# Computing qkv with the seven-product scheme of the first feed-forward matrix, and passing it to attention through DRAM

## The chip, the cores and the metric

The kernel runs on one core of a Trainium2 chip. A core has a matrix engine (PE), two engines for elementwise work (VectorE, in the profile DVE, and ScalarE, ACT), a general one (GpSimd, POOL), and a queue engine (SyncE, SP) that here does nothing but issue DMAs. The time is device microseconds of one execution, and a kernel's time is the median of its runs. Of the kernel before, three runs took 1124.48, 1124.85 and 1126.0 us.

## The reference

One transformer block over 2048 tokens of width 576, attention and feed-forward in parallel:

```
xn  = layernorm(x)
qkv = xn @ wqkv                      # 576 x 1728: q, k, v of 32 heads of 18
    # token s attends to s, s-2, ..., s-14 (8 keys, dilation 2)
    # logits * 18**-0.5, keys before token 0 masked, softmax
out = x + attention(q, k, v) @ wo + relu(xn @ w1) @ w2     # w1: 576 x 4608
```

All is float32 and is computed as such: every operand of a matrix product is split into a high and a low part (fp32r), and a product is three matmuls, high by high, low by high, high by low.

## The kernel before, in words

**Tiles.** The dilation is 2, so even and odd tokens never meet in attention. The kernel takes them as two phases of 1024 tokens; a phase is 8 tiles of 128 tokens, and a half is 4 tiles, 512 tokens. The width 576 is four blocks of 128 rows and a rest of 64.

**Feed-forward.** The 4608 hidden units are 36 tiles of 128, taken as 18 pairs. A pair and a half of the tokens is a product of a 2x2 block matrix by a 2x2 block matrix (tokens in two groups of 256 columns, hidden units in two tiles), and is done with seven block products (P1 to P7 in `pstep`) rather than eight. The weights stand still in PE and the tokens move, 256 columns in a matmul; 50 matmuls make one pair for one half. The seven slots of weights, sums and differences of the blocks, come from `set_make`: it loads a pair from a packed copy in DRAM (`w1c`), and VectorE and ScalarE form the differences in `ts` and the split parts in one of two buffers `wset`. The results are relu-ed and split by ScalarE (`hhi`) and VectorE (`hlo`), and multiplied by w2 in what is called an o-step here (`o_step`, six matmuls of 256 and 320 columns), which adds into the residual in `po`. The first pair's products are plain ones of 14 matmuls (`classic`).

**qkv.** The 32 heads are four units of 8 heads, 144 columns of each of q, k and v. In `qkv_tile` the tokens stand still in PE and the weights move: for one tile of 128 tokens and one unit, 14 matmuls of 432 columns give k, v and q with tokens on partitions. ScalarE copies the three out of the bank in three operations, into `kk`, `v` and `qo`. Four units, eight tiles and two phases make 64 such tiles. The tiles of a unit are placed between the products of one pair, at pairs 0, 3, 7, 11 and 1, 4, 8, 12 of the two phases.

**Attention.** VectorE does it, unit by unit: multiply (`pr<-qo,kk`), reduce, softmax, multiply by v, add. `kk` and `v` hold 15 slots of 144 columns on each of 128 partitions: seven slots of keys that come before the phase's tile order, then the eight tiles. Tile i and partition p is token 8p+i of the phase; the seven slots ahead hold the keys of the partition below. They are filled by the halo (`halo`, line 950): a copy within SBUF, of slots 8 to 14 of partitions 0 to 126 into slots 0 to 6 of partitions 1 to 127. It is issued as two DMAs, of 112 and of 15 partitions:

```
HALO = ((0, 112), (112, 127))
            send(lambda z=z, a=a, b=b: nc.sync.dma_start(z[a + 1 : b + 1, 0 : W - 1, :], z[a:b, NI : NI + W - 1, :]), 250, BANK["pm"])
            for z in (k, v) for a, b in HALO
```

**Order.** Every engine runs its instructions in the order written. A planner in the kernel (`Order`) writes it: it keeps a clock per engine from simple costs, puts an operation where its inputs are due, and puts attention's work on VectorE into the room that is left (`later`). `send` issues a DMA on SP's queue; an issue that waits holds every later issue of SP. `keep` puts work on POOL at the moment it is planned; the packed copies of weights are made there, by a one-element copy (`spare<-hhi`) that waits for something recent, and a DMA behind it.

Of the kernel before, what the change touches and what calls it, by code (L numbers as in the profile page):

```python
# [16 lines left out]
P = 128  # L17
# [9 lines left out]
NCL = 1  # L27
QP = ((0, 3, 7, 11), (1, 4, 8, 12))
WOP = ((5, 9, 13, 16), (6, 10, 14, 17))
HALO = ((0, 112), (112, 127))  # L30
# [12 lines left out]
class Op:  # L43


    __slots__ = ("eng", "dur", "fn", "after", "due", "end", "lag", "then")

    def __init__(self, eng, dur, fn, after, due, lag=0.0):
        self.eng, self.dur, self.fn, self.due, self.lag = eng, dur, fn, due, lag
        self.after = [a for a in after if a is not None]  # L50
        self.end = None
        self.then = None


class Order:
# [14 lines left out]
    def ready(self, op):  # L70
        r = 0.0
        for a in op.after:
            if a.end is None:
                return None
            r = max(r, a.end)
        return r

    def give(self, op, start):
        op.fn()
        self.clk[op.eng] = start + op.dur  # L80
        op.end = start + op.dur + TAIL[op.eng] + op.lag
        if op.then:
            op.then.end = self.gp = max(self.gp, op.end) + op.then.dur

# [111 lines left out]
def tile_body(ctx: ExitStack, tc: tile.TileContext, x, wqkv, wo, w1, w2, out):  # L196
# [13 lines left out]

    ctx.enter_context(tc.manual_schedule())
# [6 lines left out]
    hp = pool("hp", 5)  # L218
    whp = pool("whp", 2)
    pad3 = pool("pad3", 1).tile([P, PADS[3]], F32, name="pad3")  # L220
    vp = pool("vp", 2)
    prp = pool("prp", 2)
    lgp = pool("lgp", 1)
    smp = pool("smp", 2)
# [19 lines left out]
    BUF = [keep.tile([P, 2, 2176], F32R, name=f"wset{b}") for b in range(2)]  # L244
# [12 lines left out]
    VLAST = [[], []]  # L257

    def v_turn(last):

        o_.force(VLAST.pop(0))
        VLAST.append(last)

    def v_tile(last=None):
        v_turn([] if last is None else last)
        return vp.tile([P, 2176], F32, name="v")[:, 0 : (W - 1 + NI) * UD].rearrange("p (w c) -> p w c", w=W - 1 + NI)

    def wset(m):
        z = BUF[m % 2][:, :, 0:2048]
        return z.rearrange("p e (s k c) -> p e s k c", s=8, k=2)  # L270

    def wqset(p):
        z = BUF[(p + 1) % 2].rearrange("p e c -> p (e c)")
        return z[:, 0 : 10 * 3 * UD].rearrange("p (e t c) -> p e t c", e=2, t=5)
# [6 lines left out]
    QO, rr, RD = [None, None], [None, None], [None, None]  # L281
# [151 lines left out]
    WQC = [dram.tile([D, 3, UD], F32, name=f"wqc{u}") for u in range(NU)]  # L433
# [37 lines left out]
    TSGOT = {}  # L471

    def set_early(m):

        src = W1C[m % NP][0:256, P : 2 * P].rearrange("(k p) c -> p k c", p=P)
        TSGOT[m] = send(lambda: nc.sync.dma_start(TS[:, 1], src), 128, [*kept["w1", m % NP], *ts_free[0]])

    def set_make(m, fine=False):

        n = m % NP  # L480
        late = 0.0 if fine or m == 2 else 4.0
        aside = 5 if NP - 2 <= m < NP + 3 else 0
        w = wset(m)
        z = f32(w)[:, 1]
        got = {}
        free = slots_free(m % 2, range(8))

        def rest_rows():
            for rows in slice(0, DR), slice(DR, P):
                got[RR] = send(  # L490
                    lambda rows=rows: nc.sync.dma_start(z[rows, RR].rearrange("p k c -> p (k c)"), W1C[n][KT * P : D, :]),
                    64, [*kept["w1", n], *free], late,
                )

        for rows, f, s in ((0, 0, B11), (0, 1, B12), (256, 1, B22), (256, 0, B21)):
            if s == B12 and m in TSGOT:
                got[s] = TSGOT.pop(m)
                rest_rows()
                continue
            ts = s == B12  # L500
            dst = TS[:, 1] if ts else z[:, s]
            src = W1C[n][rows : rows + 256, f * P : (f + 1) * P].rearrange("(k p) c -> p k c", p=P)
            got[s] = send(
                lambda dst=dst, src=src: nc.sync.dma_start(dst, src), 128, [*kept["w1", n], *free, *(ts_free[0] if ts else [])], late
            )
            if s == B12:
                rest_rows()
        ok = {}

        def parts(a, b, step, src, after, slack):  # L510
            v = slice(a, b + 1, step)
            z = hi_lo(w[:, 0, v], w[:, 1, v], src, 256 * (1 + (b - a) // step), after, slack)
            for q in range(a, b + 1, step):
                ok[q] = z

        c1 = dve(lambda: sub(TS[:, 0], TS[:, 1], z[:, B11]), 256, [got[B12], got[B11]], 3 if fine else 5)
        if fine:
            parts(B11, B11, 1, z[:, B11 : B11 + 1], [got[B11], c1], 3.3)
            parts(T1, T1, 1, TS[:, 0:1], [c1], 4)
            parts(RR, RR, 1, z[:, RR : RR + 1], [got[RR]], 4.5)  # L520
        c3 = dve(lambda: sub(TS[:, 1], z[:, B22], TS[:, 1]), 256, [got[B22], c1], 5.1)
        c2 = dve(lambda: sub(TS[:, 2], z[:, B22], TS[:, 0]), 256, [c1, c3], 5.2)
        c4 = dve(lambda: sub(TS[:, 3], z[:, B21], TS[:, 2]), 256, [got[B21], c2], 5.3)
        if fine:
            parts(T2, T2, 1, TS[:, 2:3], [c2], 5.6)
            parts(B21, B21, 1, z[:, B21 : B21 + 1], [got[B21], c4], 6)
            parts(T3, T3, 1, TS[:, 1:2], [c3], 7)
            parts(B22, B22, 1, z[:, B22 : B22 + 1], [got[B22], c2, c3], 8)
            parts(T4, T4, 1, TS[:, 3:4], [c4], 9)
        else:  # L530
            parts(T1, T3, 4, TS[:, 0:2], [c1, c3], 9 + aside)
            parts(T2, T4, 4, TS[:, 2:4], [c2, c4], 10 + aside)
            parts(B11, B21, 2, z[:, B11 : B21 + 1 : 2], [got[B11], got[B21], c1, c4], 11 + aside)
            parts(B22, RR, 2, z[:, B22 : RR + 1 : 2], [got[B22], got[RR], c2, c3], 12 + aside)
        ts_free[0] = [*ok[T1], *ok[T3], *ok[T2], *ok[T4]]
        SETOK[m] = ok
# [4 lines left out]
    def w2_make(m, f):  # L541
        W2[m, f] = w = w2p.tile([P, 2, D], F32R, name="w2t")
        g = send(lambda: nc.sync.dma_start(f32(w[:, 1]), W2C[m % NP][f * P : (f + 1) * P]), 295, kept["w2", m % NP], 4.0)
        W2OK[m, f] = hi_lo(w[:, 0], w[:, 1], f32(w[:, 1]), D, [g], (24 if NP <= m < NP + 3 else 12) + 2 * f)

    WQOK = {}

    def wq_make(p, u, kts, raw=None, hold=None):

        w = wqset(p)  # L550
        b = (p + 1) % 2
        v = wqkv.rearrange("r (s c) -> r s c", s=3)[:, :, u * UD : (u + 1) * UD] if raw is not None else WQC[u]
        for kt in kts:
            z = raw[:, kt] if raw is not None else f32(w)[:, 1, kt]
            after = [] if raw is not None else list(kept["wq", u])
            free = slots_free(b, range(432 * kt // 256, min(7, (432 * kt + 431) // 256) + 1))
            if raw is None:
                after += free
            z3 = z.rearrange("p (s c) -> p s c", s=3)
            if kt < KT:  # L560
                g = [send(lambda: nc.sync.dma_start(z3, v[kt * P : (kt + 1) * P]), 221, after)]
            else:
                g = [send(lambda rows=rows: nc.sync.dma_start(z3[rows], v[KT * P : D]), 110, after)
                     for rows in (slice(0, DR), slice(DR, P))]
            if hold is not None:
                hold.append((kt, w[:, 0, kt], w[:, 1, kt], z, g))
                continue
            WQOK[p, kt] = hi_lo(w[:, 0, kt], w[:, 1, kt], z, 3 * UD, [*g, *free], 5 if p == NP + 1 else 2.5)
# [3 lines left out]
    def wo_make(ph, u):  # L572
        if u < NU:
            WO[ph, u] = w = qop[u % 2].tile([P, 2, D], F32R, name=f"qo{u % 2}")
        else:
            v_turn([])
# [3 lines left out]
        if u < NU:  # L580
            got.append(send(lambda: nc.sync.dma_start(z, WOC[u * UD : u * UD + P, :]), 295, [*kept["wo",], *turned[ph, u], *OFREE[u % 2]], 3.0))
        else:
            for b in (0, DR):
                for v in range(NU):
                    got.append(send(
                        lambda b=b, v=v: nc.sync.dma_start(z[b + 16 * v : b + 16 * v + 16], WOC[v * UD + P : (v + 1) * UD, :]),
                        37, kept["wo",], 3.0,
# [10 lines left out]
    T8 = 8 * 0.1135  # L598

    def h_alloc(key):  # L600
        H[key] = hp.tile([P, TBN], F32R, name="hhi"), hp.tile([P, TBN], F32R, name="hlo")

    def h_parts(key, src, after, slack, alloc=True):

        def high():
            h_alloc(key)
# [7 lines left out]
        a = act(high, TBN, after, slack)  # L614
        b = dve(low, TBN, [a], slack + 0.45)
        HOK[key] = [a, b]
        return [a, b]

    def terms(o, ws, xs, start):
        for j, (wp, xp_) in enumerate(((0, 0), (0, 1), (1, 0))):  # L620
            for k in range(len(ws[0])):
                mm(o, ws[wp][k], xs[xp_][k], start and j == k == 0, False)

    def rest(bank, m, f, xr):
        w = wset(m)
        for e in range(2):
            mm(bank, w[:, e, RR, f], xr, False, e == 1)

    def slot(m, s):
        w = wset(m)  # L630
        return [[w[:, e, s, k] for k in range(2)] for e in range(2)]
# [8 lines left out]
    def classic(g, j, f, name):  # L640
        ph, n, h = G[g]
        m = g // 2
# [5 lines left out]
        def f_():  # L648
            cnt = 0
            for wp, xp_ in ((0, 0), (0, 1), (1, 0)):  # L650
                for hf in range(2):
                    for k in range(2):
                        mm(bank[:, 0:TBN], first[hf][wp][k], a[hf][xp_][k], cnt == 0, False)
# [4 lines left out]
        t = pe(f_, 14 * 0.1135, [*ok[ks[0]], *ok[ks[1]], *ok[RR], *XOK[h, j], *BANK[name]])  # L658
        BANK[name] = h_parts((g, j, f), bank[:, 0:TBN], [t], 0.8)
        SETFREE[m % 2] = {q: t for q in range(8)}  # L660
# [25 lines left out]
    def pstep(g, name):  # L686
        ph, n, h = G[g]
        m = g // 2
        n2, n3 = ("bk2", "bk3") if g % 2 else ("bk3", "bk2")
# [730 lines left out]
```

## Time and profile before

| | |
|---|---|
| runs | 1124.48, 1124.85, 1126.0 us |
| span of the profiled execution, first to last instruction | 1122.7 us |
| instructions | 22406 |
| PE busy | 1116.2 us, 99% |
| VectorE busy | 825.5 us, 74% |
| ScalarE busy | 760.0 us, 68% |
| GpSimd busy | 213.1 us, 19% |
| granted PE clock, mean | 0.999 |
| DMA | 138972 packets, 115.64 MB |

The span is 1.8 to 3.3 us below the three runs; the profiled execution's own time is not listed apart from its span. In rows of groups stand the line of the kernel, the engine, the operation, output<-inputs, the shape and count, then total busy time and mean of one in ns, and the idle time before it with what ended it. Rows of the timeline and of the chain start with a start and a length in us. Most operations are recorded by helpers, so one line number (L304 matmul, L301 VectorE, L298 ScalarE) stands for many places; the tile names tell them apart.

### The profile page before, as it was taken

To read this page: it belongs to the slowest core of one execution; us is meant where nothing else is said; L and a number is where in the kernel's file an instruction comes from. 1 tells how busy PE (TensorE), PEld (TensorE's weight loads), DVE (VectorE), ACT (ScalarE), POOL (GpSimd) and SP (SyncE) were. 2 spreads that over 40 slices of the span, in tenths; PEclk is the share of its full clock that TensorE was granted. 3 is DMA by queue.
4 is the path that set the end of the run, shared out by engine and by line. 5 is a ranking of instruction groups with operands and counts; after the bars stand their busy time and mean duration, and the time that the engine had idled before them with its cause. 6 is when DMAs were issued, how large, how long until landed. Compare 5 with 4: busy or idle time off the path is not lost.

```text
span 1122.7 us, 22406 instructions
## 1 busy us (share of the span) xinstructions
PE 1116.2 (99%) x8531; PEld 1105.3 (98%) x8531; DVE 825.5 (74%) x1544; ACT 760.0 (68%) x1686; POOL 213.1 (19%) x418
## 2 busy tenths in 40 slices
PE   9999999999999999999999999999999999999998
PEld 8999999999999999999999999999999999999998
DVE  6679999944998199955881698699918994499831
ACT  6687477655776477676894676576747765677764
POOL 4343563543244122330210001001000100000000
PEclk9999999999999999999999999999999999999999
DMA  5274174364445143364461221422223222222322
GB/s 169 65 209 143 37 222 131 109 149 138 124 138 129 51 145 112 93 155 135 125 200 38 79 66 46 109 74 60 64 46 110 70 58 67 83 61 60 88 78 85
DMA packets 138972, 115.64 MB, mean 103 GB/s; under 512 B 57472, under 2 KB 117120, under 8 KB 137584
## 3 DMA queue, kind: packets, MB, share of 16 engines
q1 hardware_dynamic: 129360, 85.00, 27.4%
q0 software_dynamic: 9344, 28.91, 8.8%
q8 instruction: 67, 1.10, 0.4%
q10 hardware_dynamic: 160, 0.30, 0.1%
q14 instruction: 41, 0.34, 0.1%
HBM read 96.01 MB, written 36.50 MB: 118 GB/s over the span
## 4 chain that ended last, share of the span: by engine, by line
PE 97%; DMA 1%; ACT 1%; SPq 1%; DVE 0%; issue 0%; ACTq 0%
PE po L304 45%; PE bk L304 31%; PE pm L304 15%; PE bkA L304 6%; DMA kk<-in_wqkv 1%; DMA x<-in_x 0%; PE pm L374 0%; DVE wset L301 0%; SPq L1256 0%; ACT xs L298 0%; ACT x L298 0%; PE bk L374 0%; SPq L1241 0%; ACT po L298 0%; SPq L1252 0%
## 5 line engine op out<-in xcount | busy, mean ns | idle before, releaser
L304 PE MATMUL po<-w2t,hhi 128*128 128x256 f32 (+1 forms) x2304 | 394.3, 292 | 0.0
L304 PEld LDWEIGHTS po<-w2t,hhi 128*128 128x128 f32 x2304 | 334.2, 188 | 0.7
L298 ACT ACTIVATE x<-po 128x576 f32<-128x576 f32 x286 | 186.0, 651 | 177.5 <-PE po L304 174.2
L304 PE MATMUL po<-w2t,hlo 128*128 128x256 f32 (+1 forms) x1152 | 243.2, 292 | 0.0
L304 PE MATMUL bk<-xs,wset 128*128 128x256 f32 x1680 | 238.1, 277 | 0.0
L304 PEld LDWEIGHTS bk<-xs,wset 128*128 128x128 f32 x1680 | 217.2, 188 | 0.7 <-DVE hlo L612 0.2
L298 ACT ACTIVATE po<-x 128x576 f32<-128x576 f32 x286 | 187.0, 654 | 5.6
L304 PEld LDWEIGHTS po<-w2t,hlo 128*128 128x128 f32 x1152 | 189.6, 187 | 0.0
L304 PE MATMUL pm<-wset,xa 128*128 128x432 f32 x744 | 165.8, 359 | 0.0
L304 PEld LDWEIGHTS pm<-wset,xa 128*128 128x128 f32 x744 | 136.2, 188 | 6.0 <-ACT qo L298 0.4
L443 POOL COPY spare<-hhi 1x1 f32<-1x1 f32 x176 | 82.6, 469 | 273.6 <-ACT hhi L298 273.6
L304 PE MATMUL bk<-xa,wset 128*128 128x256 f32 x876 | 124.1, 278 | 0.0
L301 DVE TENSOR_TENSOR sn<-bk,sn 128x256 f32<-128x256 f32 x140 | 59.1, 422 | 79.9 <-PE bk L304 46.6
L304 PEld LDWEIGHTS bk<-xa,wset 128*128 128x128 f32 x876 | 113.2, 188 | 0.6 <-ACT xa L298 0.3
L298 ACT ACTIVATE kk<-pm 128x144 f32<-128x144 f32 (+1 forms) x66 | 20.5, 310 | 113.8 <-PE pm L304 113.6
L301 DVE TENSOR_TENSOR w2t<-w2t 128x576 fp32r<-128x576 f32 (+1 forms) x72 | 54.1, 752 | 58.7 <-ACT w2t L298 57.3
L983 POOL TENSOR_SCALAR_AFFINE_SELECT lg<-lg 1x512 f32<-1x512 f32 x8 | 9.5, 1194 | 438.9 <-DVE lg L980 438.9
L1009 DVE TENSOR_TENSOR pr<-lg,v 128x1152 f32<-128x1152 f32 x64 | 85.2, 1352 | 0.2
L977 DVE TENSOR_TENSOR pr<-qo,kk 128x1152 f32<-128x1152 f32 x64 | 85.1, 1350 | 0.0
L980 DVE TENSOR_REDUCE lg<-pr 128x64 f32<-128x1152 f32 x64 | 84.4, 1345 | 0.5
L304 PE MATMUL bk<-xr,wset 128*128 128x256 f32 x426 | 83.1, 277 | 0.0
L301 DVE TENSOR_TENSOR wset<-wset 128x512 fp32r<-128x512 f32 (+2 forms) x121 | 71.5, 592 | 9.1 <-ACT wset L298 7.6
(157 smaller groups left out, 1556.2 us busy)
## 6 DMA issues: line engine op xcount, KB each, us to landing
w2t<-w2c SPq DMA_DIRECT2D x70, 288.0 KB, 3.0
wset<-w1c SPq DMA_DIRECT2D x105, 128.0 KB, 2.6
w1c<-in_w POOLq DMA_DIRECT2D x72, 144.0 KB, 2.8
w2c<-in_w POOLq DMA_DIRECT2D x72, 144.0 KB, 3.2
wset<-wqc SPq DMA_DIRECT2D x28, 216.0 KB, 2.6
out<-x SPq DMA_DIRECT2D x16, 288.0 KB, 2.1
ts<-w1c SPq DMA_DIRECT2D x35, 128.0 KB, 2.7
wset<-w1c SPq DMA_DIRECT2D x70, 64.0 KB, 2.2
```

Source lines behind the costliest of these rows:

```text
L298: nc.scalar.activation(o, i, func)
L301: nc.vector.tensor_tensor(o, a, b, op=op)
L304: nc.tensor.matmul(o, l, r, start=start, stop=stop, skip_group_check=True)
L443: nc.gpsimd.tensor_copy(spare[0:1], f32(LATEST[-1])[0:1, 0:1])
L977: nc.vector.tensor_tensor(pr[i], q, window(k, i), op=ALU.mult)
L980: nc.vector.tensor_reduce(s["lg"][:, i], pr.pop(i).rearrange(heads, d=Dh), axis=AX.X, op=ALU.add)
L983: nc.gpsimd.affine_select(out=z, in_=z, pattern=[[1, NI], [1, W], [0, HG]], compare_op=ALU.is_ge, fill=-1e9 / scale, base=1 - W, channel_m ...
L1009: nc.vector.tensor_tensor(pr[i].rearrange(heads, d=Dh), e, window(v, i).rearrange(heads, d=Dh), op=ALU.mult)
```

## The change

qkv's 1728 columns are seven more pairs of tiles, six of 256 columns and one of 192 ("Q sets"). Each is computed as a pair of w1 is, with weights standing still, in a `wset` buffer, with its seven slots made by `set_make`. A phase now has 25 sets, F for w1 and Q for wqkv, in the order F0 Q0 Q1 F1 Q2 F2 Q3 F3 Q4 F4 Q5 F5 Q6 F6 ... F17. The first phase's Q0 is done by plain products at the start. o-steps are spread over the half sets that follow, so that those of a few F sets also fill the Q sets.

A Q product comes out with columns of qkv on partitions. VectorE turns it in blocks of 32x32 into one of four buffers `stg`, and four DMAs write that to a scratch in DRAM (`qd`). When the columns of a unit are all there, `unit` and `fetch` load k, q and v of the unit from the scratch into `kk`, `qo` and `v`, the tiles in two pieces of 128 partitions and the halo in one of 127 partitions. A unit's 144 columns can lie in two Q sets, and then there are twice as many pieces. The packed copy of wqkv (`wqc`) is now one per Q set; where a set's columns come from several of q, k and v and units, each range is a copy of its own, so that a set takes 4 to 16 copies.

The loads on SP around the first unit of attention, before (the two buffers' loads, `w2t` loads, and the halo):

```order
L543 DMA w2t_841<-w2c1_201 128x576
L543 DMA w2t_843<-w2c1_201 128x576
L950 DMA kk_134<-kk_134 112x1008
L950 DMA kk_134<-kk_134 15x1008
L950 DMA v_423<-v_423 112x1008
L950 DMA v_423<-v_423 15x1008
L504 DMA wset0_132<-w1c2_184 128x2x128
L504 DMA ts_135<-w1c2_184 128x2x128
```

and of the change, where the fetch of the whole unit stands ahead of the loads of the set of pair 2:

```order
L1055 DMA kk_150<-qd0_0_241 127x7x128
L1055 DMA kk_150<-qd0_0_241 128x4x128 x2
L1055 DMA kk_150<-qd0_1_242 127x7x16
L1055 DMA kk_150<-qd0_1_242 128x4x16 x2
L1055 DMA qo0_1246<-qd0_0_241 128x4x128 x2
L1055 DMA qo0_1246<-qd0_1_242 128x4x16 x2
L1055 DMA v_1247<-qd0_1_242 127x7x144
L1055 DMA v_1247<-qd0_1_242 128x4x144 x2
L532 DMA wset1_139<-w1c2_200 128x2x128
L532 DMA ts_151<-w1c2_200 128x2x128
```

Before, two copies of 1008 elements a row filled each halo from SBUF; now one copy of 127 rows, seven slots and 128, 16 or 144 columns fills it from DRAM. The set's loads stand behind it in both.

The start of POOL's queue, before: the layernorm's `rstd` and `nm` of the last two tiles of tokens (tiles 6 and 7) and then the first packed copies.

```order
L346 TENSOR_TENSOR rstd_551<-mv_550,mhalf_112 128x1
L349 TENSOR_SCALAR nm_555<-mv_550,rstd_551 128x1
L346 TENSOR_TENSOR rstd_593<-mv_592,mhalf_112 128x1
L349 TENSOR_SCALAR nm_597<-mv_592,rstd_593 128x1
L443 COPY spare_114<-hhi_687 1x1
L444 DMA w1c1_183<-in_w1 144x256
```

and of the change, the last two of the sixteen pairs of copy and DMA for the second Q set, and the same tiles 6 and 7 behind them:

```order
L476 COPY spare_120<-hb1_142 1x1
L477 DMA wqc1_235<-in_wqkv 144x144
L476 COPY spare_120<-hb1_142 1x1
L477 DMA wqc1_235<-in_wqkv 144x80
L378 TENSOR_TENSOR rstd_596<-mv_595,mhalf_118 128x1
L381 TENSOR_SCALAR nm_600<-mv_595,rstd_596 128x1
L378 TENSOR_TENSOR rstd_647<-mv_646,mhalf_118 128x1
L381 TENSOR_SCALAR nm_651<-mv_646,rstd_647 128x1
```

ScalarE waits for `nm_600` in the first of these rows, and the fifth, which PE's products for tokens 512 to 1023 read, stands behind it:

```order
L389 ACTIVATE pr_627<-x6_127,nm_600,rstd_596 128x576
L330 ACTIVATE x2_123<-po0_154 128x576
L330 ACTIVATE xr0_135<-sn5_152 64x256
L330 ACTIVATE x3_124<-po1_155 128x576
L330 ACTIVATE xa10_131<-bk3_158 128x4x128
```

The sixteen pairs moved ahead of the layernorm of tiles 6 and 7.

The diff, cut to what is spoken of:

```diff
-QP = ((0, 3, 7, 11), (1, 4, 8, 12))
-WOP = ((5, 9, 13, 16), (6, 10, 14, 17))
-HALO = ((0, 112), (112, 127))
+NQ = 7
+QPOS = ((1, 2, 4, 6, 8, 10, 12), (1, 2, 4, 6, 8, 10, 12))
+WOLAST = (16, 17)
+NHB = 6
+NST = 4
...
-    def wq_keep(u, z):
-        rows = slice(96 * z, 96 * (z + 1))
-        src = wqkv.rearrange("r (s c) -> r s c", s=3)[rows, :, u * UD : (u + 1) * UD]
-        kept_part(("wq", u), WQC[u][rows], src, 166)
+    def wq_keep(q, z):
+        rows = slice(144 * z, 144 * (z + 1))
+        for off, src, cnt in SEGS[q]:
+            kept_part(("wq", q), WQC[q][rows, off : off + cnt], wqkv[rows, src : src + cnt], 0.576 * cnt)
...
+    def q_out(t, j, f, src, after, slack):
...
+        def turn():
...
+            nc.vector.transpose(got[0][0:wd, j], src[0:wd])
+
+        op = dve(turn, TBN, [*after, *before], slack)
...
+            for a in range(wd // 32):
+                dst = QD[ph, q][4 * h : 4 * h + 4, :, f * wd + 32 * a : f * wd + 32 * (a + 1)]
+                e = send(
+                    lambda: nc.sync.dma_start(
+                        dst.rearrange("i (b r) c -> r (i b) c", r=32),
+                        z[32 * a : 32 * (a + 1)].rearrange("r j (z c) -> r (j z) c", c=32),
+                    ), 80, ops,
+                )
...
+    def fetch(ph, u, part, dst, after, got, halo=True):
+        lst = []
+        for q, off, c0, cnt in PIECES[part, u]:
+            src = QD[ph, q][:, :, off : off + cnt]
+            to = dst[:, :, c0 : c0 + cnt]
+            if halo:
+                lst.append((to[1:P, 0 : W - 1], src[1:NI, 0 : P - 1], cnt))
+            for a in range(0, NI, NI // 2):
+                b = (W - 1) * halo
+                lst.append((to[:, a + b : a + b + NI // 2], src[a : a + NI // 2], cnt))
...
+            z = send(lambda: nc.sync.dma_start(o, i.rearrange("i p c -> p i c")), cnt * 2, after)
...
-    qkv_tile(0, 0, 0)
+    tq = 2 * SQ0
+    classic(tq, 0, 0, "pm")
     turn_one(3)
-    qkv_tile(0, 0, 1, "bk2")
+    classic(tq, 0, 1, "bk2")
     classic(0, 1, 0, "pm")
     classic(0, 1, 1, "bkA")
+    keep_set(2)
     turn_one(4, name="bk2")
     out_four(0, 1)
     turn_one(5)
     s0 = s_forms(0, 30)
-    qkv_tile(0, 0, 2)
+    classic(tq, 1, 0, "pm")
     classic(1, 0, 0, "bk2")
     classic(1, 0, 1, "bkA")
+    keep_set(3)
     turn_one(6, name="bk2")
-    qkv_tile(0, 0, 3)
+    classic(tq, 1, 1, "pm")
     turn_one(7)
...
-        cnt = {"P1": l0 // 2, "P6": l0 - l0 // 2, "P7": l1 // 2, "P3": l1 - l1 // 2}
+        todo = -(-len(queue) // (nxt - t + 1))
...
+            if name in SHARE:
+                for _ in range(todo * (SHARE[name] + 1) // 4 - todo * SHARE[name] // 4):
+                    o_step(*queue.popleft())
+                    tick()
```

`keep_set(s)` makes the packed copy of set s on POOL. `turn_one(i)` normalises tile i and turns it so that the width lies on partitions.

More of the change, by code (lines that the diff above doesn't have):

```diff
@@ L543, in w2_make @@
         g = send(lambda: nc.sync.dma_start(f32(w[:, 1]), W2C[m % NP][f * P : (f + 1) * P]), 295, kept["w2", m % NP], 4.0)
[L544 to L568, printed above, removed]
+        W2OK[m, f] = hi_lo(w[:, 0], w[:, 1], f32(w[:, 1]), D, [g], (7 if SETS[SF[m] - 1][1] == "Q" else 24 if NP <= m < NP + 3 else 12) + 2 * f)
     WO, WOOK = {}, {}
@@ L598, in tile_body, with stub, h_parts @@
     T8 = 8 * 0.1135
[L600 to L603 removed]
+    T3B = [TG[GP] - 4, TG[GP] + 3]
+    def stub():
+        return Op(SP, 0.0, None, (), 0.0)
+    HBFREE = [(0.0, b) for b in range(NHB)]
+    HUSED = {}
+    def h_parts(key, src, after, slack):
         def high():
[L606 removed]
+            HBFREE.sort()
+            HUSED[key] = b = HBFREE.pop(0)[1]
+            H[key] = HB[b][:, 0], HB[b][:, 1]
             LATEST.append(H[key][0])
@@ L947, in halo, with known @@
-    def halo(p, u):
-        k, v = KK, VV[u % 2]
-        HALOOK[p] = [
-            send(lambda z=z, a=a, b=b: nc.sync.dma_start(z[a + 1 : b + 1, 0 : W - 1, :], z[a:b, NI : NI + W - 1, :]), 250, BANK["pm"])
-            for z in (k, v) for a, b in HALO
-        ]
-        attention(p // NP, u, HALOOK[p])
-    def attention(ph, u, halo):
-        qo, k, v = QO[u % 2], KK, VV[u % 2]
+    VDONE = []
+    OFREE = [[], []]
+    OUTS = {}
+    POLL = []
+    def known(ops):
+        return all(z.end is not None and z.end <= o_.now() + 0.3 for z in ops)
@@ new lines, in fetch_poll, with unit, k_in, v_in @@
+    def fetch_poll():
+        while FETCH and (o_.dma < o_.now() + 2.0):
+            o, i, cnt, after, got = FETCH.pop(0)
+            z = send(lambda: nc.sync.dma_start(o, i.rearrange("i p c -> p i c")), cnt * 2, after)
+            if got:
+                got.end = z.end
+    def unit(ph, u):
+        kl, vl, ql = stub(), stub(), stub()
+        there = [z for q in range(QNEED[u] + 1) for z in QOUT[ph, q]]
+        def k_in():
+            nc.gpsimd.memset(KK[0:1, 0 : W - 1, :], 0.0)
+            fetch(ph, u, 1, KK, there, kl)
+        def v_in():
+            VV[u % 2] = v_tile()
+            nc.gpsimd.memset(VV[u % 2][0:1, 0 : W - 1, :], 0.0)
+            fetch(ph, u, 2, VV[u % 2], there, vl)
+        def q_in():
+            QO[u % 2] = q_raw(u % 2).rearrange("p (i c) -> p i c", i=NI)
+            fetch(ph, u, 0, QO[u % 2], there, ql, False)
+        poll([*there, *KFREE[0]], k_in)
+        poll([*there, *([WODONE[ph, u - 2]] if u > 1 else OFREE[u])], q_in)
+        poll([*there, *VDONE], v_in)
+        return attention(ph, u, kl, vl, ql)
@@ L957, in attention @@
+    def attention(ph, u, kl, vl, ql):
+        k = KK
         heads = "p w (h d) -> p w h d"
@@ L1392, in tile_body @@
+    idx_now[:] = [2 * NS, 0]
+    while queue:
+        o_step(*queue.popleft())
+        tick()
+    run_plan(99)
+    plan.pop(2 * NS, None)
     o_.finish()
```

672 lines of the change are left out of this document (382 added, 290 removed).

## The prediction

> **What bounds the kernel now.** I read the page first, then the waits of PE:
>
> ```profile
> span 1122.7 us, 22406 instructions
> PE 1116.2 (99%) x8531; PEld 1105.3 (98%) x8531; DVE 825.5 (74%) x1544; ACT 760.0 (68%) x1686; POOL 213.1 (19%) x418
> PE 97%; DMA 1%; ACT 1%; SPq 1%; DVE 0%; issue 0%; ACTq 0%
> PE po L289 <- POOL mhalf L236: 1.4, 1, 1.4
> ```
>
> PE is busy for 1116.2 of 1122.7 us and makes 97% of the chain that ended last; its longest wait is 1.4 us. So the time is PE's work, and whatever stops PE adds to it in full, since nothing idle is there to take it up. VectorE has 297 us of room and ScalarE 363, spread over the span.
>
> **PE's work: what is removed and added.** The groups of the qkv matmuls, and two pieces of the chain of waits, a qkv tile (432 columns, 14 matmuls) and a plain product (256 columns, 14):
>
> ```profile
> L304 PE MATMUL pm<-wset,xa 128*128 128x432 f32 x744 | 165.8, 359 | 0.0
> L304 PE MATMUL pm<-wset,xr 128*128 128x432 f32 x124 | 43.5, 360 | 0.1
> L304 PE MATMUL bk<-wset,xa 128*128 128x432 f32 x24 | 5.5, 365 | 0.0
> L304 PE MATMUL bk<-wset,xr 128*128 128x432 f32 x4 | 1.4, 356 | 0.0
> ...
> 70.88 1.59 PE bk L304 x14
> ...
> 117.80 2.75 PE pm L304 x14
> ```
>
> 744+124+24+4 = 896 = 64 tiles x 14. A mean of 359 ns includes the overlap of neighbours, so I take the pieces: 64 x 2.75 = 176.0 us go. What comes: of fourteen Q sets, thirteen by seven products for two halves, 50 matmuls each, 13 x 100 = 1300, and the first by plain products, 8 x 14 = 112; 1412 matmuls at 1.59/14 = 0.1136 us are 160.4 us. **PE saves 15.6 us**; its other work stays. That is the whole possible gain, and the rest is what could stop PE.
>
> **VectorE, ScalarE.**
>
> ```profile
> L1023 DVE STREAM_TRANSPOSE pr<-qo 128x128 f32<-128x128 f32 x64 | 13.6, 274 | 0.0
> L1050 DVE STREAM_TRANSPOSE pr<-pr 128x64 f32<-128x64 f32 x16 | 2.3, 208 | 0.0
> L301 DVE TENSOR_TENSOR sn<-bk,sn 128x256 f32<-128x256 f32 x140 | 59.1, 422 | 79.9 <-PE bk L304 46.6
> 644.49 0.69 DVE L301 TENSOR_TENSOR wset<-ts,wset 128x512 fp32r<-128x512 f32 x1
> ...
> L301 DVE TENSOR_TENSOR wset<-kk,wset 128x432 fp32r<-128x432 f32 x5 | 2.7, 602 | 0.0
> L298 ACT ACTIVATE kk<-pm 128x144 f32<-128x144 f32 (+1 forms) x66 | 20.5, 310 | 113.8 <-PE pm L304 113.6
> ```
>
> 112 turns of 128x256 are new. 64 columns more cost 66 ns between the first two rows; 128 more than the first give 274 + 132 = 406 ns (at most twice 274): 45 us. Thirteen sets by products add 52 sums at 0.42 and 52 differences as long, 44 us, and 80 low parts at 0.69, 55 us; the old low parts of wqkv (35 of 128x432, 0.60) and 56 of 128x256 (0.42) go, 45 us. So VectorE gains about 100 us and stands near 925 of 1110, 83%: no bound. ScalarE loses 192 copies of some 0.3 us and gains about as much. I cost both at nothing; their cover is PE's queue of o-steps, and the price without it is a rival below.
>
> **POOL at the start.** The sixteen copy-and-DMA pairs of the second Q set now stand ahead of the layernorm of tiles 6 and 7. Before, the first twelve such pairs ran behind it:
>
> ```profile
> 23.76 0.27 POOL L349 TENSOR_SCALAR nm<-mv,rstd 128x1 f32<-128x1 f32 x1
> 28.94 0.55 POOL L346 TENSOR_TENSOR rstd<-mv,mhalf 128x1 f32<-128x1 f32 x1 [4.92 <-DVE mv L345]
> ...
> 38.70 0.18 POOL L443 COPY spare<-hhi 1x1 f32<-1x1 f32 x1 [4.92 <-ACT hhi L298]
> ...
> 47.22 0.54 POOL L444 DMA_DIRECT2D w1c<-in_w  x1
> 34.57 1.57 PE L304 MATMUL bk<-xa,wset 128*128 128x256 f32 x12
> ```
>
> Twelve took 38.70 to 47.76, 0.755 each; sixteen take 12.1 us. They can start when tile 5's `nm` is done (24.0), so tile 6's `rstd` comes at 36.1 instead of 28.94. ScalarE waits for it in `pr<-x6`, and the `xa10` that the products for tokens 512 to 1023 read stands behind that: with about 3 us for `rstd`, `nm`, `pr` and the split, 39.2. PE reached those products at 34.57, and now, with three qkv tiles ahead of them 1.15 us shorter each, could at 31.1. The stall is at most 8.1 us, and nothing if the pairs start earlier than their copies' source allows me to see; I take **7 us**.
>
> **Thin cover of the products.** Before, eight o-steps of six matmuls stood among a half set's products; in the Q sets it is two or three. Where none stands between P1 and P6, ScalarE must copy P1's sum while PE does P5:
>
> ```profile
> 613.85 0.87 PE L304 MATMUL bk<-xa,wset 128*128 128x256 f32 x6
> 614.55 1.74 PE L304 MATMUL pm<-wset,xa 128*128 128x432 f32 x8
> 614.75 0.37 ACT L298 ACTIVATE bkA<-bk 128x256 f32<-128x256 f32 x1 [0.32 <-PE bk L304]
> 636.59 0.65 ACT L298 ACTIVATE x<-po 128x576 f32<-128x576 f32 x1 [1.03 <-PE po L304]
> ```
>
> P1 leaves PE at 614.55, its copy ends at 615.12, 0.57 later; P5 is eight matmuls, 0.91 us. So 0.34 us are spare, and ScalarE in the middle of a 0.65 us operation costs up to 0.31. Over some 50 half sets (26 Q ones, and F ones beside them with as few) that is 0 to 15.5 us; ScalarE is free a third of the time, and mostly hits the spare part: **2 us**.
>
> **The halo.** This decides. Before, seven slots of 127 partitions went in copies of 112 and of 15 partitions; now in one of 127, and out of 7 x 127 = 889 runs of 144, 128, 96, 48 or 16 columns. The queues and the landings:
>
> ```profile
> q1 hardware_dynamic: 129360, 85.00, 27.4%
> q0 software_dynamic: 9344, 28.91, 8.8%
> wset<-w1c SPq DMA_DIRECT2D x105, 128.0 KB, 2.6
> kk<-kk SPq DMA_DIRECT2D x8, 441.0 KB, 4.4
> kk<-kk SPq DMA_DIRECT2D x8, 59.1 KB, 3.9
> ```
>
> A packet of q1 (SP's queue) has 657 B on the mean and took 0.274 x 16 x 1122.7 / 129360 = 38.0 ns of one DMA engine; one of q0 has 3094 B and took 169 ns. The line through both is 2.7 ns and 0.0538 ns a byte. So a halo of 144 columns, 512 KB, is 889 x (2.7 + 31.0) = 30 us of one engine, and all 16 of them (in 26 pieces, 8.19 MB) 441 + 62 = **503 us of one engine**. Spread over sixteen, that is 2 us a halo and lost in the landing; the 441 KB above landed in 4.4 us, so that copy was spread, for one engine needs 26 us for it. All on one engine, a halo takes 30 us there.
>
> No row has a copy of 127 rows. 128, 64, 32 and 16 rows, and 112 and 15, can be dealt out in equal shares of whole rows to 8 to 16 engines; 127 is a prime, and equal shares need one engine or 127. The nearest rows by size say spread (4.4 us); by the count of rows, every copy in this trace has a count that divides, and the only ones with an odd span, the halos, were cut so that both parts do. I take the one-engine side, at 0.78: it needs only that rows are dealt equally.
>
> The Trainium skill ("DMA: Bandwidth & Descriptors", under the semaphore that counts to 16, the paragraph on how many engines) says that the copy uses the largest number up to 16 that divides the slowest dimension on both sides, and names 127 partitions as a case of one engine. By that rule the sum is the one that follows; without it, 1118.3. The trace agrees as far as 112 rows being spread.
>
> Everything later on SP's queue has a share on that engine too, and waits behind it. What is late next is the set that loads behind the fetch. How much slack it has, from a set of before:
>
> ```profile
> 633.24 0.37 SPq L504 DMA_DIRECT2D ts<-w1c  x1
> 635.18 1.35 DVE L977 TENSOR_TENSOR pr<-qo,kk 128x1152 f32<-128x1152 f32 x1
> 640.48 0.42 DVE L301 TENSOR_TENSOR ts<-ts,wset 128x256 f32<-128x256 f32 x1
> 664.38 0.42 DVE L301 TENSOR_TENSOR ts<-ts,wset 128x256 f32<-128x256 f32 x1
> ```
>
> The load is issued at 633.24 and VectorE uses it at 640.48; less 2.6 for the landing, 4.6 us are spare. Then VectorE stands still, and with it the sums and low parts that PE's banks wait for: some 2 us later PE stops too. So about 7 us of a burst are hidden when the loads stand right behind it, and more when the fetch goes out earlier in the set's 23.9 us (640.48 to 664.38), half of it, 12 us, on the mean. A phase has seven bursts (k and v of the first unit go out together, 60 us; the others, k and v apart, about 30 each). Of 503 us, 14 x 7 = 98 are hidden at the least, which leaves 405; with 12 more each, 237. I take the middle, **320 us**. The first unit's k is read by VectorE soon after its fetch, which makes for the upper end; the other units' k and v are read long after, so for them only the loads count.
>
> The 216 writes of the scratch and some 90 other fetches are shared copies like `turned<-pr`, and are hidden: an issue takes SP a few tenths, as the 0.37 above.
>
> **The sum.** Against the span: 1122.7 - 15.6 + 7 + 2 + 320 = 1436. The runs are 2.15 us above it by their median: **1438 us**.
>
> **The rivals.**
>
> *A: the halo is spread* (faster). For it: the 4.4 us of 112 rows, and DMA engines that are busy for little more than a third (27.4% + 8.8%). Against it: the prime count. Then 1124.85 - 15.6 + 7 + 2 = 1118.3 us. It decides from a halo that lands under 12 us.
>
> *B: spread, and the start has its cover too.* POOL's pairs cost nothing because PE has other work there, and the products are covered: 1109.3 us. Against it: the chain at the start is PE with no wait, so no other work is there.
>
> *C: spread, and the thin cover costs its full price* (slower). In each of the 50 half sets ScalarE is in an `x<-po` when P1 ends: 15.5 us, with the start 1131.8. It decides from (15.6 - 7) / 50 = 0.17 us a half set. For it: ScalarE's order has a 0.65 us operation with each o-step. Against it: fewer o-steps also mean fewer of these.
>
> **How the numbers follow.** One engine 0.78, A 0.13, B 0.04, C 0.05. The one-engine case alone runs from 1124.85 - 15.6 + 237 = 1346 to 1124.85 - 15.6 + 9 + 405 = 1523; to leave out no more than 2 in 10 the range has to reach to A, so it is 1116 to 1540. This kernel's runs lie 0.13% apart, so that 0.2%, 2.2 us, is about what can be told from no change. Faster by more: A and B, less a part of A with a larger stall at the start, 0.14. Within: that part and some of C, 0.04. Slower: the forecast and the rest of C, 0.82.
>
> **What would show it.** Right: `kk<-qd` and `v<-qd` with landings of 25 us and more, loads of `wset` behind them with the same; PE waits of about 320 us, in some fourteen groups, ended by VectorE or by ScalarE which wait for a DMA of a set; PE busy near 1102 us; one wait of about 7 us between 31 and 40 us, ended by ScalarE's `xa`, with POOL in the pairs; the turns of 128x256 near 0.41 us. Wrong: `kk<-qd` landing in 5 us throughout, and PE without waits after 50 us. If the landings are long but PE's waits are small, the slack of a set is what I have too small; if PE waits for more than 400 us, other things on the queue, the turns' buffers or attention on VectorE, are late as well.

## The result, and the profile after

The changed kernel takes 1464.02 us (four runs, 1462.02 to 1466.4) against 1124.87 before: 1.301 times as long, 95% interval 1.2991 to 1.3028. The forecast was 1438. The profiled execution took 1462.02 us, with a span of 1460.2. First the page:

```profile
span 1460.2 us, 24167 instructions
PE 1142.4 (78%) x9047; PEld 1135.6 (78%) x9047; DVE 911.4 (62%) x1749; ACT 757.5 (52%) x1561; POOL 262.2 (18%) x522
PE   7961894859393966999999719965986596979998
PEclk9985897979696988999999959988997898989999
PE 50%; SPq 32%; DVE 7%; DMA 4%; ACT 3%; issue 2%; POOL 1%; DVEq 0%; ACTq 0%; POOLq 0%
```

PE, busy in every slice before, now has holes. PE's busy time and what is left of the span make the whole account: 1142.4 + 317.8. Before it was 1116.2 + 6.5. So 311 us are waiting, and PE is busy 26 us longer although by the forecast it has 15.6 us less to do. The waits of PE, in total and by their longest:

```profile
PE bk L336 <- DVE sn L333: 161.3, 9, 25.4
PE bk L336 <- ACT sn L330: 47.3, 3, 24.3
PE pm L336 <- ACT sn L330: 47.0, 3, 28.4
PE po L336 <- ACT po L330: 28.1, 2, 15.7
PE pm L336 <- DVE sn L333: 19.2, 1, 19.2
PE bk L336 <- ACT xa L330: 5.7, 1, 5.7
```

Nineteen waits make almost all of it. The engines named here wait themselves: of VectorE's waits two are large.

```profile
DVE ts L333 <- DMA ts<-w1c: 160.4, 9, 23.8
DVE pr L1103 <- DMA qo<-qd: 94.5, 4, 30.5
```

A set of weights comes late nine times, and attention's first operation of a unit four times. Why they are late stands in SP's part of the timeline, around the first unit (a start, a length, the queue, the line, the copy and how many):

```profile
83.78 1.03 SPq L532 DMA_DIRECT2D wset<-wqc  x2
84.86 35.08 SPq L1055 DMA_DIRECT2D kk<-qd  x6
120.04 2.10 SPq L1055 DMA_DIRECT2D qo<-qd  x4
122.18 23.08 SPq L1055 DMA_DIRECT2D v<-qd  x3
145.43 0.67 SPq L532 DMA_DIRECT2D wset<-w1c  x1
```

with the first two copies of this fetch and of the next one by themselves, from shorter stretches of the same view,

```profile
84.86 0.36 SPq L1055 DMA_DIRECT2D kk<-qd  x1
85.28 24.08 SPq L1055 DMA_DIRECT2D kk<-qd  x1
...
206.27 0.32 SPq L1055 DMA_DIRECT2D kk<-qd  x1
206.64 27.61 SPq L1055 DMA_DIRECT2D kk<-qd  x1
```

and PE at that place:

```profile
126.50 1.65 PE L336 MATMUL pm<-xs,wset 128*128 128x256 f32 x6 [28.44 <-ACT sn L330]
127.95 1.64 PE L336 MATMUL po<-w2t,hb 128*128 128x256 f32 x6
129.39 1.48 PE L336 MATMUL bk<-xs,wset 128*128 128x256 f32 x6
130.67 0.63 PE L336 MATMUL bk<-xr,wset 128*128 128x256 f32 x2
131.10 1.10 PE L336 MATMUL po<-w2t,hb 128*128 128x256 f32 x6
132.04 0.85 PE L336 MATMUL pm<-xa,wset 128*128 128x256 f32 x6
```

The halo piece is the first copy of a fetch, and its own issue is the short one: 0.2 to 1.0 us in all 26 pieces. It is the copy behind it, of 128 partitions, that SP cannot issue for 6 to 28 us, where an issue took 0.4 before. By the marks that the copies leave in the trace when they complete, the two halo pieces land 28.2 and 32.1 us after their issue, 3.8 and 4.1 us after SP is let go. The set of weights stands behind all this and isn't issued until then.

And when PE is let go at 126.50, six matmuls take 1.45 us from start to start, and from 132.04 on 0.69: for 4.6 us after a wait PE runs at half speed. A row over these 4.6 us shows it (length, busy time of the engines, then the granted PE clock, the busy share of the sixteen DMA engines, and GB/s):

```profile
126.50:131.10 4.60, 4.59 (x21) 4.60 (x22) 4.57 (x6) 1.31 (x2) 0.00 (x0) 0.50 0.07 22
```

The clock is 0.50. In the same stretch `v`'s halo is on its way, and the DMA engines are busy for 0.07 of the time, which is about one of sixteen.

### The profile page after: what moved, and what is told of

Read it like the earlier page. It is cut to its first block, busy times and chain, and to the rows that moved or that the text cites. A ratio compares the mean times of both kernels' runs of the same rounds, so it can differ in the third digit from the quotient of the medians.

```text
span 1460.2 us, 24167 instructions
## 1 busy us (share of the span) xinstructions
PE 1142.4 (78%) x9047; PEld 1135.6 (78%) x9047; DVE 911.4 (62%) x1749; ACT 757.5 (52%) x1561; POOL 262.2 (18%) x522
## 4 chain that ended last, share of the span: by engine, by line
PE 50%; SPq 32%; DVE 7%; DMA 4%; ACT 3%; issue 2%; POOL 1%; DVEq 0%; ACTq 0%; POOLq 0%
SPq L1055 30%; PE po L336 23%; PE bk L336 16%; PE pm L336 7%; PE bkA L336 4%; DVE pr L1135 2%; DMA ts<-w1c 1%; DVE pr L1142 1%; SPq L532 1%; DMA qo<-qd 1%; DMA wset<-w1c 1%; DMA w2t<-w2c 1%; ACT x L330 1%; DVE sn L333 1%; DVE hb L623 1%
## 5 line engine op out<-in xcount | busy, mean ns | idle before, releaser
L336 PE MATMUL po<-w2t,hb 128*128 128x256 f32 (+1 forms) x3456 | 516.6, 297 | 28.1 <-ACT po L330 28.1
L336 PEld LDWEIGHTS po<-w2t,hb 128*128 128x128 f32 x3456 | 476.7, 192 | 28.5 <-ACT po L330 28.5
L336 PE MATMUL bk<-xs,wset 128*128 128x256 f32 (+1 forms) x1596 | 231.4, 282 | 47.9 <-ACT sn L330 47.3
L336 PE MATMUL bk<-xa,wset 128*128 128x256 f32 (+1 forms) x864 | 132.8, 293 | 167.5 <-DVE sn L333 161.3
L336 PEld LDWEIGHTS bk<-xa,wset 128*128 128x128 f32 (+1 forms) x864 | 119.6, 201 | 170.2 <-DVE sn L333 163.2
L336 PEld LDWEIGHTS bk<-xs,wset 128*128 128x128 f32 (+1 forms) x1596 | 209.6, 191 | 48.7 <-ACT sn L330 47.9
L476 POOL COPY spare<-hb 1x1 f32<-1x1 f32 x228 | 107.9, 473 | 378.4 <-ACT hb L330 372.9
L1103 DVE TENSOR_TENSOR pr<-qo,kk 128x1152 f32<-128x1152 f32 x64 | 85.5, 1347 | 94.6 <-DMA qo<-qd 94.5
L336 PE MATMUL pm<-xs,wset 128*128 128x256 f32 (+1 forms) x708 | 103.8, 283 | 47.0 <-ACT sn L330 47.0
L336 PEld LDWEIGHTS pm<-xs,wset 128*128 128x128 f32 (+1 forms) x708 | 93.7, 193 | 47.8 <-ACT sn L330 47.6
L336 PE MATMUL bkA<-xa,wset 128*128 128x256 f32 (+1 forms) x624 | 88.8, 279 | 0.5 <-ACT bkA L330 0.5
```

Source lines behind the costliest of these rows:

```text
L336: nc.tensor.matmul(o, l, r, start=start, stop=stop, skip_group_check=True)
L476: nc.gpsimd.tensor_copy(spare[0:1], f32(LATEST[-1])[0:1, 0:1])
L1103: nc.vector.tensor_tensor(pr[i], q, window(k, i), op=ALU.mult)
```

## The experiments

### 1 and 2. The halo cut at 112, and at 113

The change with its halo piece cut in two, once at 112 partitions as the kernel before did it, once at 113:

```diff
             if halo:
-                lst.append((to[1:P, 0 : W - 1], src[1:NI, 0 : P - 1], cnt))
+                for a, b in ((0, 112), (112, 127)):     # the other: ((0, 113), (113, 127))
+                    lst.append((to[a + 1 : b + 1, 0 : W - 1], src[1:NI, a:b], cnt))
```

> The changed kernel, but each halo piece goes in two DMAs, of 112 and of 15 partitions, as the halo did before. Theory (a copy of 127 rows runs on one DMA engine): each of the 26 pairs lands in about 5 us, the long waits of PE vanish, its granted clock goes back to 0.99, and what is left is PE's saving of 15.6 us less the wait at the start (5.7 + 0.9 us idle, some 2.5 us more from a lower clock behind it): 1124.9 - 15.6 + 9 = 1118 us, 1114 to 1122. Rival (the way through DRAM is what stalls: its 216 writes in runs of 128 bytes, or reads right behind writes): still above 1300 us, since nothing of that is touched.

> As the last, but split at 113 instead of 112: copies of 113 and of 14 partitions. 113 is a prime as 127 is. Theory (equal shares of whole rows, so one engine for a prime count): a halo of 144 columns holds SP for 113/127 of 27.6 us, 24.6 us; of the 339 us that the change lost, less the 9 at the start, about (330 - 14 x 3) are left: 1380 to 1430 us. Rival (any cut in two helps, because each copy is shorter or needs fewer descriptors): as with the cut at 112, about 1118 us.

Cut at 112, it took 1126.0 us (ten runs, 1123.46 to 1128.74), 1.0014 of before (1.0004 to 1.0023). Cut at 113, one run, 1419.24. The page, landings and a wait of the first, then SP's issues of `kk` and the page of the second:

```profile
span 1121.6 us, 24206 instructions
PE 1104.5 (98%) x9047; PEld 1100.7 (98%) x9047; DVE 911.2 (81%) x1749; ACT 757.1 (67%) x1561; POOL 246.4 (22%) x522
kk<-qd SPq DMA_DIRECT2D x2, 441.0 KB, 4.7
PE bk L336 <- ACT xa L330: 5.6, 1, 5.6
```

```profile
span 1417.5 us, 24206 instructions
L1056 SPq DMA_DIRECT2D kk<-qd x56: 284/468/25364, 86.3 to 1191.0; - x56
```

One row more in the first of two copies, and the kernel is 293 us slower. The longest issue, of a copy that stands behind a piece of 113 rows, is 25.4 us (expected 24.6), while 112 rows with almost the same bytes, from the same scratch, land in 4.7. It is the count of rows: 127 and 113 are primes, 112 is 7 x 16. The marks of completion say the same without any time: copies of 112 and of 15 rows leave 16 of them, of 14 rows 15, and of 113 or 127 rows 2, one soon after the issue and one at the landing. That fits one mark for each engine that does a share, and one more for the rest where they aren't sixteen. A count above 16 that is neither a prime nor a multiple of 16 was not run. The way through DRAM, common to both, isn't the cause of the loss. The first expectation, 1118, was missed by 8 us, however: with the halo put right the change gains nothing.

### 3. The kernel before with one copy of 127 rows

```diff
-HALO = ((0, 112), (112, 127))
+HALO = ((0, 127),)
```

> The kernel before, with its halo within SBUF in one DMA of 127 partitions instead of 112 + 15. There a row is one run of 4032 bytes, so a halo has 127 runs, not 889. Theory (one engine, whose time goes by bytes): 127 x (2.7 + 0.0538 x 4032) = 28 us a halo, 56 for k and v together; less about 10 hidden, eight times 46, and 2.3 us a time for the lower clock: 1125 + 386 = 1510 us, 1420 to 1570. Rival (the price is SP's, about 31 ns for each run that it issues): 127 runs cost 4 us, all hidden: 1125 to 1130 us.

One run: 1383.86 us. The rows of SP's timeline around the first unit:

```profile
59.78 0.73 SPq L950 DMA_DIRECT2D kk<-kk  x1
60.62 9.76 SPq L950 DMA_DIRECT2D v<-v  x1
70.55 21.46 SPq L504 DMA_DIRECT2D wset<-w1c  x1
92.11 2.34 SPq L504 DMA_DIRECT2D ts<-w1c  x1
```

The loss is there without any of the rest of the change, which settles the place. The rival, a price that SP pays for each run, falls: 127 runs of 4032 bytes hold the queue as well. But the size was wrong, 259 us instead of 386. By the marks of completion the second of two halos lands 42 to 48 us after the first one's issue, where I had 56; PE waits 235 us at the eight places, 29 us each, where I had 46. Packets of 4032 bytes start 153 ns apart here, where I had 220 for a run. In the change, where a halo runs alone, they start 7.1 ns apart at 64 bytes, 24 at 512 and 26 at 576: the prediction's line through the means of two queues is too steep.

SP is held as in the change: the halo's own issue takes 0.73 us, the next ones wait. How much is in flight seems to have a limit. Where a single halo is on its way, SP is let go 1.0 to 1.1 us before its landing with runs of 64 bytes, 4.1 to 4.6 with 576, and 13 to 16 with 4032. By the distances of the packets that is at most some 150, 180 and 105 runs still to go, an estimate, so the limit seems to count runs and not bytes. That was not tried.

The wait that the prediction told of, at the busy engine itself, shows here too: of the set's copy that SP begins to issue at 70.55, fifteen marks of completion are there by 93.76, and the sixteenth comes at 106.78, just behind the landing of `v`'s halo at 106.42.

### 4. The first burst of each phase alone

The cut at 112 for units 1 to 3, the single copy for unit 0:

```diff
-                for a, b in ((0, 112), (112, 127)):
+                for a, b in ((0, 127),) if u == 0 else ((0, 112), (112, 127)):
```

> The cut at 112 for the halos of units 1 to 3, the single copy of 127 rows only for unit 0 of each phase. Theory (each burst costs what PE waits for it, plus the lower clock behind it, and the bursts add up): the four waits of the change at 98 to 152 us and at 829 to 879 us, 28.4 + 18.5 + 24.3 + 19.3 = 90.5 us, and four times 2.3 us: 1126 + 100 = 1226 us, 1210 to 1240. Rival (a late first unit makes everything after it late, and the later bursts cost little by themselves): clearly more than 1300 us.

One run: 1222.03 us. The waits of the change at those places and the lower clock behind them explain it to 4 us: the bursts are local, and add up.

### 5. The halo on GpSimd's queue

```diff
+            eng = nc.gpsimd if o.shape[0] == P - 1 else nc.sync
-            z = send(lambda: nc.sync.dma_start(o, i.rearrange("i p c -> p i c")), cnt * 2, after)
+            z = send(lambda: eng.dma_start(o, i.rearrange("i p c -> p i c")), cnt * 2, after)
```

> The changed kernel with the halo copies of 127 rows issued by GpSimd instead of SP; all else, the copies' shape too, as in the change. Theory (the copy runs on one engine, and the harm is done because everything else on SP's queue stands behind it): with a queue of its own the copy still lands late if it is on one engine, about 25 us, but sets and turned results go past it; only attention's first operation of a unit waits, most at the first unit of each phase: 1126 to 1190 us. Rival (one busy DMA engine is enough to hold every copy that has a share there, whatever the queue): near 1460 us. The Trainium skill ("DMA: Bandwidth & Descriptors", how many engines) names GpSimd's queue as an exception that may spread 127 rows over all sixteen; then the landing is some 5 us, and the time is that of the cut, about 1126 us.

One run: 1429.88 us. The landings of the halo, and two waits behind it, of attention and, for a copy that SP had issued at 156.71, of ScalarE:

```profile
kk<-qd POOLq DMA_DIRECT2D x2, 500.1 KB, 37.4
v<-qd POOLq DMA_DIRECT2D x4, 500.1 KB, 34.6
```

```profile
142.13 1.36 DVE L1104 TENSOR_TENSOR pr<-qo,kk 128x1152 f32<-128x1152 f32 x1 [47.73 <-DMA kk<-qd]
180.46 0.68 ACT L330 ACTIVATE w2t<-w2t 128x576 fp32r<-128x576 f32 x1 [20.10 <-DMA w2t<-w2c]
```

The theory's range is missed by far, and the rival was right, or nearly. The copies of GpSimd are no faster: a halo of 144 columns lands in 34 to 38 us, 8 of which are its issue, so the exception that the Trainium skill allows for this queue ("DMA: Bandwidth & Descriptors", how many engines: it may spread 127 rows over all sixteen) isn't seen for this copy. And another queue does not protect SP's: the w2 tile, which SP begins to issue at 156.71, has fifteen marks of completion by 170.46 and the sixteenth only at 180.44, behind the landing of `v`'s halo at 177.09. The median landing of such a tile in this run is 3.5 us. Part of the loss is new, since GpSimd issues the second piece of `kk` only when the first has landed (at 119.77 and 119.34) and attention waits 48 us. How the 304 us divide between the two was not measured.

### 6 and 7. The start

What was left of the loss after the cut: the sixteen pairs of copy and DMA on GpSimd. Once they and the next set's were put behind the layernorm of tiles 6 and 7; once each range of a set became one DMA of 576 rows, four pairs instead of sixteen, at the old place.

```diff
     classic(0, 1, 1, "bkA")
-    keep_set(2)
...
     turn_one(7)
+    keep_set(2)
+    keep_set(3)
     keep_set(4)
```

> The cut at 112, and the packed copies of the second Q set and of the set after it on GpSimd behind the layernorm of tiles 6 and 7, where the first copies stood before. Theory (the sixteen pairs ahead of it hold PE at the start): PE's wait of 5.7 us at 38 us and the lower clock behind it go, 7 to 9 us less than with the cut alone: 1110 us, 1107 to 1113. Rival (the second Q set's copy is needed that early, and comes late now): no gain against the cut alone, and a wait of PE for the set at 55 to 70 us instead.

```diff
     def wq_keep(q, z):
-        rows = slice(144 * z, 144 * (z + 1))
+        if z:
+            return
         for off, src, cnt in SEGS[q]:
-            kept_part(("wq", q), WQC[q][rows, off : off + cnt], wqkv[rows, src : src + cnt], 0.576 * cnt)
+            kept_part(("wq", q), WQC[q][:, off : off + cnt], wqkv[:, src : src + cnt], 2.304 * cnt)
```

> The cut at 112, and each range of a Q set's packed copy in one DMA of 576 rows instead of four of 144: 4 pairs of copy and DMA for the second Q set instead of 16, still ahead of the layernorm of tiles 6 and 7. Theory (what is left of the loss after the cut is the start, where either the layernorm or the second Q set comes late): the pairs end at 26 us, before tile 6's statistics are there (28 us), and the set is in DRAM 8 us earlier, so that both waits go: 7 to 10 us less than with the cut alone, 1116 to 1119 us. Rival (the rest of the loss is thin cover, spread over the span): 1124 to 1127 us, as with the cut alone. Rival (a DMA of 576 rows costs GpSimd four times one of 144): the pairs end where they did, 1126 us.

First the change itself, where the pairs run from 23.09 to 34.5 and PE waits:

```profile
23.09 0.18 POOL L476 COPY spare<-hb 1x1 f32<-1x1 f32 x1
33.95 0.53 POOL L477 DMA_DIRECT2D wqc<-in_wqkv  x1
34.50 0.58 POOL L378 TENSOR_TENSOR rstd<-mv,mhalf 128x1 f32<-128x1 f32 x1
38.24 2.93 PE L336 MATMUL bk<-xa,wset 128*128 128x256 f32 x12 [5.75 <-ACT xa L330]
```

Put behind, 1125.24 us, 1.0002 of before (0.9993 to 1.0012), and no clear gain on the cut alone. The first wait is gone, and the rival's has come:

```profile
60.73 1.62 PE L336 MATMUL pm<-xs,wset 128*128 128x256 f32 x6 [3.20 <-ACT wset L330]
73.40 1.17 PE L336 MATMUL pm<-xs,wset 128*128 128x256 f32 x6 [2.83 <-ACT sn L330]
```

Merged, 1120.35 us (five runs, 1119.48 to 1122.77), **0.9962 of before (0.9948 to 0.9975)**: this version is a little faster than both kernels, by 0.4% against the one before. The four pairs end before the statistics of tile 6 are there; a DMA of 576 rows keeps GpSimd 0.64 us, one of 144 rows 0.53:

```profile
25.46 0.64 POOL L477 DMA_DIRECT2D wqc<-in_wqkv  x1
27.45 0.56 POOL L378 TENSOR_TENSOR rstd<-mv,mhalf 128x1 f32<-128x1 f32 x1 [1.34 <-DVE mv L377]
```

It was expected at 1116 to 1119, a little too low. What PE still waits for, by its totals:

```profile
span 1118.6 us, 24050 instructions
PE 1103.3 (99%) x9047; PEld 1098.7 (98%) x9047; DVE 910.9 (81%) x1749; ACT 755.7 (68%) x1561; POOL 215.1 (19%) x408
PE pm L336 <- DVE sn L333: 1.8, 1, 1.8
PE bk L336 <- ACT sn L330: 1.5, 2, 1.1
PE pm L336 <- ACT sn L330: 1.1, 1, 1.1
```

### 8. The Q sets further apart

```diff
-QPOS = ((1, 2, 4, 6, 8, 10, 12), (1, 2, 4, 6, 8, 10, 12))
+QPOS = ((1, 2, 4, 7, 10, 13, 16), (1, 2, 4, 7, 10, 13, 16))
```

> The kernel with the cut at 112 and the merged packed copies, and the Q sets further apart: at 1, 2, 4, 7, 10, 13, 16 of the 25 sets instead of 1, 2, 4, 6, 8, 10, 12, so that two F sets instead of one lie between them and each half set has more o-steps. Theory (what is still missing is thin cover: waits of PE for ScalarE's and VectorE's sums, some 6 us after the first 60 us): 2 to 4 us less, 1116.5 to 1118.5 us. Rival (those waits come from attention's work in VectorE's order, which only moves with the Q sets): 1119 to 1122 us, no change; with attention pressed into less time they may grow.

1139.84 us, 1.0138 of before (1.0121 to 1.0155). The small waits hardly changed: behind the first 60 us and outside 480 to 510 us they sum to 3.6 us, against 4.2 in run 7, so this run doesn't bear the theory out. Between 480 and 510 us, at the end of the first phase, larger ones came:

```profile
484.89 1.65 PE L336 MATMUL pm<-xs,wset 128*128 128x256 f32 x6 [4.14 <-ACT sn L330]
502.16 1.65 PE L336 MATMUL pm<-xa,wset 128*128 128x256 f32 x6 [8.45 <-DVE sn L333]
```

The last unit's attention starts later and presses on the out-projection there: VectorE waits 8.0 us, until 500.7, for a load of attention's output, and the sums that PE needs stand behind it. What the wider spacing adds here is the lateness of attention. A schedule that spreads only the second phase was not tried.

## Why the prediction was right, point by point

**The halo on one engine: right.** It was the forecast's main case, and runs 1 to 3 show that the count of rows is the cause, with a prime beside 112 and in the kernel before. The 0.07 of the DMA engines and the two marks of completion show the one engine itself. The rule of the Trainium skill on how many engines a copy uses ("DMA: Bandwidth & Descriptors", the section on why a DMA increments its semaphore by 16) agrees with the halo copies that SP issued: 127 and 113 rows with 2 marks and slow, 112 with 16 and fast, 15 and 14 rows with 16 and 15. The time of these small ones would not tell, since their 98 or 105 runs take 3 us at most on one engine, an estimate by 26 ns each.

**Its size: right, with one more place of waiting than told.** I had 503 us of one engine and 320 us of it bare. By the marks of completion the 26 pieces land 515 us after their issues in sum, those of 144 columns after 26 to 32 us, as I had named for the sign (the profile lists no landing of SP's queue in this run). A part of the agreement is luck: by the distances of the packets the bare time of the engine is some 410 us, an estimate, and what the landings have above that was not divided. PE's waits at the bursts are 302 us: 47 and 44 us for the first unit of the two phases, and 11 to 25 for each of twelve others. The range of 237 to 405 holds it, and the middle was near. What I had not seen is where the copies behind a halo wait. I had them all issued, and waiting on that engine; in the change SP can't issue the next copy until the halo is within some microseconds of its landing, and the chain gives 29.7% of the span to this line. Run 3 shows both waits. Attention's first operation waited as well, 94.5 us in four places, at the first and the last unit of each phase, where I had it only for the first. (The other fetches are 76, not some 90; the sum has no term for them.)

**PE's work: the missing term.** The forecast made PE busy for 1116.2 - 15.6 = 1100.6 us; it was 1142.4. With the halo cut it is 1104.5. The 38 us between are the half-speed stretches behind sixteen waits, 2.4 us each; PE is busy for 71 us of them at a granted clock of 0.50, which makes 35 of the 38. The rows at 126.50 show one, and the 2.93 us for twelve matmuls at 38.24 the same behind the wait at the start. Run 4 has four such waits and 10.5 us more (1115.0 against 1104.5), run 3 ten and 23.7 more. My step was "whatever stops PE adds to it in full"; it adds more than that. The Trainium skill ("TensorE: Matmul & The Clock Gate", Part 1) says so: after an idle window of about 3.4 us PE's clock is halved, until it has been busy for about as long. The trace agrees, with 4.6 us at half speed behind the first burst, but in run 6 a wait of 2.83 us, shorter than that window, was enough; I did not put it into the sum. The account: idle time 317.8 against 335.5 forecast (6.5 of before, 7, 2 and 320), busy time 41.8 more, of which 38 are this term; the difference is the 24 us between 1436 and 1460.

**The start: the right place, the size a little low.** Sixteen pairs took 11.4 us (12.1 forecast), and PE waited 5.75 us for `xa10` as told (7 forecast); with the lower clock behind it the gain from taking it away was 5.65 us between the two medians, 1126.0 and 1120.35, and 3.0 us between the two profiled executions, the first of which was the fastest of its ten.

**Thin cover: too low.** I took 2 us. In the merged version PE's waits behind the first 60 us are 6 us, in places of up to 1.8 us, for VectorE's sums as much as for ScalarE's copies. Run 8 doesn't show that it is thin cover that makes them.

**VectorE** was forecast at 925 us and is 911; a turn of 128x256 takes 440 ns, not 406:

```profile
L651 DVE STREAM_TRANSPOSE stg<-sn 128x256 f32<-128x256 f32 (+1 forms) x52 | 22.7, 440 | 1.0
```

**Rival A** (the halo spread, 1118.3 us) can be read off run 1: 1126.0. Its terms were the saved work less 9 us. PE's busy time fell by 11.7 us, not 15.6: 1.2 us more went with the wait at the start (1103.3 in run 7), the rest was not traced. Idle time grew by 10.6 us: 7.8 in the first 80 us, the rest small waits behind them. The median of its runs is 2.5 us above the profiled one.

## What to carry to other kernels

Before a copy's shape is changed, look at the row count of its outer dimension: 112 and 15 rows land in 5 us where 127 rows take up to 32 and hold SP's next issue for up to 28. In these runs a burst's wait of PE cost about 2.4 us on top of itself. A small helper DMA that is multiplied by four may cost more by its place in an engine's order than by its bytes: by the medians merging them was worth 5.7 us, and moving them no clear gain.

## What the runs showed of the hardware that was not expected

- Behind a copy that one engine carries, SP's next issue took up to 27.6 us, while the copy's own issue took 0.2 to 1.0 us; with 127 runs of 4032 bytes it took 0.73 us and the next two 9.8 and 21.5.
- On the one engine packets start 7.1 ns apart at 64 bytes, 24 at 512, 26 at 576 and 153 at 4032; the line through the means of the two queues, 2.7 ns and 0.0538 ns a byte, is fair for the first (6.1) and too high for the last two (33.7 and 220).
- One engine that was busy with GpSimd's copy held the last sixteenth of a copy of SP's for 10 us after the other fifteen, 23.7 us after its issue: a second queue was no way around it.
- GpSimd spends 8.0 us on issuing a copy of 889 runs, whether of 64 or of 576 bytes, and 0.64 on one of 576 runs in one range.
- A wait of PE of 2.83 us was enough for the half clock (run 6, from 74.0 to 77.4 us); one of 1.78 us was not (run 7, at 88.4).
